# A fused chunk attention and two-layer MLP kernel: the first tile's reciprocals spread by fp32 TensorE transposes, its last k copies split over two engines

## The chip, the core and the metric

The kernel runs on one core of one Trainium2 chip. The time is device microseconds of one execution; "before" has a median of 291.13 us over the three runs that were there at the start (290.92 to 292.19).

## The reference, cut to what matters

```python
# q, k, v: 8 batches x 8 heads x 576 x 64, chunks of 64
scores = scale * q_c @ k_c.T            # within each chunk
attn = exp(scores - max); attn = attn / (attn.sum(-1) + 1e-9)
x = (attn @ v_c) -> (4608 tokens, 512)
out = gelu_exact(x @ w_in) @ w_out      # w_in 512 x 2048, w_out 2048 x 512
```

The tokens are worked through in nine tiles of 512. A tile has four "pairs" of heads (0 to 3). While one tile's MLP keeps TensorE busy, the attention of the next tile is slipped in between. Only the first tile's attention stands alone at the start, with nothing to hide behind.

## The kernel before

For one pair, the first tile does: transpose q and k; copy them out of PSUM, where the matmuls put their results (`qT`, and `k_bd`, a block-diagonal k in two halves of 64 partitions); scores `s_ps`; `pT = exp`; the sums of pT; their reciprocals, spread over 64 partitions each (`rc`); the product with v (`av_ps`); `x = av_ps * rc`. Then come the MLP's h slots: 16 slots of four matmuls each over x 0 to 3.

Pairs 0 and 1 get their reciprocals by VectorE, pairs 2 and 3 by TensorE:

```python
def att_sum(t, g, ...):                       # pairs 0, 1
    nc.tensor.matmul(sum_ps[:], ones_bd[:], pT[:], ...)
    nc.vector.transpose(t1, sum_ps)           # 32x32 blocks
    nc.vector.reciprocal(r1, t1[:, :, 0])
    nc.vector.transpose(rc, r1 broadcast)
def att_sum_pe(t, g):                         # pairs 2, 3
    for m in range(4):
        nc.tensor.matmul(sT[:, m], pT[..m..], ones_r[:], ...)    # sums, 2 columns
    nc.vector.reciprocal(rr[:], sT[:])
    def spread():                             # called later by the schedule
        for m in range(4):
            for r in range(2):
                nc.tensor.matmul(rc_ps[64*r:64*(r+1), m*128:(m+1)*128],
                                 rr[:, m, r:r+1].to_broadcast([128, 64]), ident_f[:],
                                 tile_position=(0, 64*r), ...)
        nc.scalar.copy(rc, rc_ps)
```

The schedule of the first tile is written out by hand (S_ scores, T transposes and copies, U reciprocals, A products with v, AC ScalarE, DV VectorE, PO GpSimd; `keep_warm(n)` issues n matmuls whose result nobody reads):

```python
S_[1]()
cast_qk(0, "q", 3, DV)
U[0]()
T[5](); T[6](); T[7]()          # k 2, q 3, k 3; k copied by AC
U[1]()
S_[2](); keep_warm(1); S_[3](); keep_warm(1)
p2 = att_sum_pe(0, 2); p3 = att_sum_pe(0, 3)
A[0](); p2(); A[1](); p3(); A[2](); keep_warm(1); A[3]()
# ... cut: loads
for i, eng in enumerate((PO, AC, DV, PO)):
    win[0](i, eng)              # casts of w_in for slots 0 to 3
act_table(Act.Gelu)
```

The whole kernel:

The softmax here doesn't subtract the row's maximum and nothing guards it: scores larger than these inputs give would overflow.

Of the kernel before, what the change touches and what calls it, by code (L numbers as in the profile page):

```python
# [11 lines left out]
def kernel(  # L12
# [137 lines left out]
        copy(qT[:].rearrange("p i (c j) -> p i c j", j=J), tp)  # L150
        tiles[t]["qT", g] = qT

    def att_Tk(t, g, copy):
        tp = transposed(t, "k", g)
        for r in range(2):
            sl = slice(CH * r, CH * (r + 1))
            copy(k_bds[g][sl, :, sl].rearrange("p i (c j) -> p i c j", j=J), tp[sl])  # L157


    def flip(t, nm):  # L160
# [101 lines left out]
    def att_sum_pe(t, g):  # L262

        pT = tiles[t]["pT", g]
        sT = ps_at.tile([P, MT // P, 2], f32, tag="at", name="sT")
        for m in range(MT // P):
            nc.tensor.matmul(sT[:, m], pT[:].rearrange("p i c -> p (i c)")[:, m * P:(m + 1) * P], ones_r[:],
                             start=True, stop=True)
        rr = work.tile([P, MT // P, 2], f32, tag="rr", name="rr", bufs=2)
        nc.vector.reciprocal(rr[:], sT[:])  # L270

        def spread():
            rc_ps = ps_mm.tile([P, MT], f32, tag="mm", name="rc_ps")
            for m in range(MT // P):
                for r in range(2):
                    nc.tensor.matmul(rc_ps[CH * r:CH * (r + 1), m * P:(m + 1) * P],  # L276
                                     rr[:, m, r:r + 1].to_broadcast([P, D]), ident_f[:],
                                     start=True, stop=True, tile_position=(0, CH * r))
            rc = work.tile([P, NB, 32], f32, tag="rc", name="rc", bufs=4)
            nc.scalar.copy(rc[:].rearrange("p n e -> p (n e)"), rc_ps[:])  # L280
            tiles[t]["rc", g] = rc
        return spread

# [17 lines left out]
    def att_units(t, cq=DV, ck=DV):  # L301
        tiles[t]["x"] = xpool.tile([P, G, MT], bf16, tag="x", name="x")
        T = []
        for g in range(G):
            T += [lambda g=g: att_Tq(t, g, cq), lambda g=g: att_Tk(t, g, ck if t == 0 or g < 2 else DV)]
        S_ = [lambda g=g: att_S(t, g) for g in range(G)]
        if t > 1:
            T = [lambda g=g: flip_k(t, g, ck) for g in range(G)]
            S_ = [lambda g=g: (att_S_flipped(t, g), att_part(t, g)) for g in range(G)]
        if t > 0:  # L310
            U = [lambda g=g: att_total(t, g, g + 2) for g in (0, 2)] + [lambda g=g: att_rc(t, g) for g in range(G)]
        else:
            U = [lambda g=g: att_sum(t, g) for g in range(G)]
        A = [lambda g=g: att_av(t, g) for g in range(G)]
        return T, S_, U, A
# [71 lines left out]
    def phase(t, extra1, extra2, by_rows=False, between={}):  # L387
        nms = MT // P
        order = [(ms, qt) for ms in range(nms) for qt in range(NQ)]
        if by_rows:  # L390
            order = [(None, f) for f in range(FF - FC)] + [(ms, NQ - 1) for ms in range(nms)]
        first = 3 if t == 1 else 1
        mm1_slot(t, 0, first, between)
        for f in range(first, FF):
            for u in extra1.get(f, ()):
                u()
            mm1_slot(t, f)
        for s, (ms, qt) in enumerate(order):
            for u in extra2.get(s, ()):
                u()  # L400
            if ms is None:
                mm2_rows(t, qt)
            else:
                mm2_slot(t, ms, qt)
        for u in extra2.get("end", ()):
            u()
# [43 lines left out]
    with tc.manual_schedule():  # L450
        for g in range(G):
            for nm in "qk":
                load_qk(0, nm, 2 * g, 2 * g + 2)
        load_v(0)
        win = [load_w_in(c, 2 if c < 2 else 1) for c in range(NWC - 1)]
        act_table(Act.Exp)
        keep_warm(7)
        zero_k(k_bds[0], nc.gpsimd)
        zero_k(k_bds[1], nc.gpsimd)
        zero_v(0, nc.vector)  # L460
        T, S_, U, A = att_units(0, DV, AC)
        cast_qk(0, "k", 0, PO)
        zero_k(k_bds[2], nc.gpsimd)
        cast_qk(0, "k", 1, PO)
        zero_k(k_bds[3], nc.gpsimd)
        cast_qk(0, "k", 2, PO)
        cast_qk(0, "k", 3, PO)
        for g in range(G):
            cast_v(0, 0, PO, slice(g, g + 1))
            cast_v(0, 1, PO, slice(g, g + 1))  # L470
        cast_qk(0, "q", 0, DV)
        T[0]()
        cast_qk(0, "q", 1, DV)
        T[1]()
        keep_warm(3)
        T[2]()
        S_[0]()
        T[3]()
        cast_qk(0, "q", 2, DV)
        keep_warm(1)  # L480
        T[4]()
        keep_warm(1)
        S_[1]()
        cast_qk(0, "q", 3, DV)
        U[0]()
        T[5]()
        T[6]()
        T[7]()
        U[1]()
        S_[2]()  # L490
        keep_warm(1)
        S_[3]()
        keep_warm(1)
        p2 = att_sum_pe(0, 2)
        p3 = att_sum_pe(0, 3)
        A[0]()
        p2()
        A[1]()
        p3()
        A[2]()  # L500
        keep_warm(1)
        A[3]()
        win.append(load_w_in(NWC - 1))
        wout = [load_w_out(0)]
        for i, eng in enumerate((PO, AC, DV, PO)):
            win[0](i, eng)
        act_table(Act.Gelu)
        load_qk(1, "q")
        wout.append(load_w_out(1))
        for c in range(1, NWC):  # L510
            for i in range(4):
                win[c](i, DV if i % 2 == 0 else PO)
            if c == 1:
                load_qk(1, "k")
            else:
                wout.append(load_w_out(c))
            if c < 3:
                r = slice(CH * (c - 1), CH * c)
                o = slice(CH * (2 - c), CH * (3 - c))
                nc.gpsimd.memset(v_bds[1][r, :, :, o], 0.0)  # L520
        for i in range(FC):
            wout[0](i, DV if i % 2 == 0 else PO)
        load_v(1)
        for g in range(G):
            cast_qk(1, "q", g, DV if g == 0 else PO)
        for i in range(FC):
            wout[1](i, DV if i % 2 == 0 else PO)
        for g in range(G):
            cast_qk(1, "k", g, DV if g % 2 == 0 else PO)
        for i in range(FC):  # L530
            wout[2](i, PO)
        for i in range(2):
            wout[3](i, PO)
        for g in range(G):
            for r in range(2):
                cast_v(1, r, PO, slice(g, g + 1))

        T, S_, U, A = att_units(1, AC, AC)
        def next_qk():
            for nm in "qk":  # L540
                load_qk(2, nm)
        over = []

        def sums():
            over.append(att_sums(1))
            over[0](1)
        phase(0, {}, {0: [lambda: act_table(Act.Exp)],
                      2: [T[0]], 3: [T[2]], 4: [T[4], T[6]], 7: [T[1], T[3]], 8: [T[5], S_[0]],
                      9: [T[7], S_[1], next_qk], 10: [S_[2], lambda: att_sum(1, 0), lambda: wout[3](2, DV)],
                      11: [lambda: wout[3](3, AC), S_[3]], 12: [sums],  # L550
                      13: [A[0], lambda: over[0](2), lambda: over[0](3), U[3]], 14: [A[1], U[4]], 15: [A[2], U[5]]},
              by_rows=True)
        last_av = {1: [A[3], lambda: rows_out(0, 3)]}
        pool_cast_qk(2)
        for t in range(1, NT):
            nxt = t + 1 < NT
            if nxt:
                T, S_, U, A = att_units(t + 1)
                for nm in "qk":
                    flip(t + 1, nm)  # L560
                if t == 1:
                    load_v(2)
                for r in range(2):
                    cast_v(t + 1, r, PO)
                if t + 2 < NT:
                    load_all(t + 2)
                    pool_cast_qk(t + 2)
            e1, e2 = {}, {}
            if nxt:
                e1 = {8: [T[0]], 10: [T[1]], 12: [T[2]], 14: [T[3]]}  # L570
                e2 = {0: [lambda: act_table(Act.Exp), S_[0]], 1: [S_[1]], 2: [S_[2]],
                      3: [S_[3], U[0]], 5: [U[1], lambda: act_table(Act.Gelu)],
                      7: [U[2], A[0]], 8: [U[3], A[1]], 10: [U[4], A[2]], 12: [U[5], A[3]]}
            phase(t, e1, e2, between=last_av if t == 1 else {})
# [28 lines left out]
```

## Time and profile before

| | before |
|---|---|
| time, median | 291.13 us |
| TensorE busy | 278.2 us, 96% of the span |
| score matmuls of pair 1 begin ("S1") | 9.42 us |
| scores of pair 3 begin | 12.77 us |
| x of pair 3 done | 18.52 us |
| long run of h matmuls begins | 18.56 us, 3 of 64 done |

The last four rows are from TensorE's and VectorE's timelines.

### The profile page before, as it was taken

How to read it: one execution, taken by the hardware profiler on the slowest of the kernel's cores; microseconds unless marked ns; L12 is line 12 of the kernel's file. 1: busy time of each engine (PE TensorE's matmuls, PEld its weight loads, DVE VectorE, ACT ScalarE, POOL GpSimd, SP SyncE). 2: the span in 40 equal slices, each digit the busy share in tenths (PEclk: the TensorE clock that was granted, in tenths of full speed). 3: DMA queues.
4: the chain of work that ended last, by engine and by line, in shares of the span. 5: the costliest groups of instructions: out<-in, count | busy, mean ns of one | idle time of the engine just before them, and what ended most of it. 6: DMA issues, size and time to landing. Idle time of an engine off the chain costs nothing.

```text
span 288.9 us, 4859 instructions
## 1 busy us (share of the span) xinstructions
PE 278.2 (96%) x1836; PEld 138.5 (48%) x1870; DVE 154.8 (54%) x265; ACT 170.1 (59%) x329; POOL 98.8 (34%) x136
## 2 busy tenths in 40 slices
PE   7699999999999999999999999999999999999994
PEld 2454455445544554455445544554455445544444
DVE  6854349348805882749246935394268425850011
ACT  3767766967447844785468536763785368626400
POOL 6859758605651830262008400650003610000000
PEclk9999999999999999999999999999999999999999
DMA  6999999999799726961698259914999970120033
GB/s 222 247 360 404 393 337 265 254 207 286 191 291 311 168 99 161 325 145 74 161 261 234 76 138 285 233 73 115 163 130 131 265 147 2 39 106 2 0 73 73
DMA packets 96887, 53.79 MB, mean 186 GB/s; under 512 B 68576, under 2 KB 89312, under 8 KB 96864
## 3 DMA queue, kind: packets, MB, share of 16 engines
q1 hardware_dynamic: 96704, 53.36, 69.8%
q8 instruction: 14, 0.23, 0.3%
q10 hardware_dynamic: 160, 0.13, 0.2%
q14 instruction: 9, 0.07, 0.1%
HBM read 36.70 MB, written 9.44 MB: 160 GB/s over the span
## 4 chain that ended last, share of the span: by engine, by line
PE 90%; DVE 3%; ACT 3%; DMA 2%; issue 1%; SPq 0%; POOL 0%; DVEq 0%; POOLq 0%
PE h_ps L328 42%; PE y_ps L344 37%; PE av_ps L289 3%; PE y_ps L384 3%; PE s_ps L180 2%; DMA arrival<-in_k_dram 2%; ACT k_bd L157 2%; PE y_ps L369 1%; DVE x L296 1%; PE tp L144 1%; PE rc_ps L276 1%; DVE rc L259 1%; ACT pT L194 1%; SPq L112 0%; PE s_ps L192 0%
## 5 line engine op out<-in xcount | busy, mean ns | idle before, releaser
L328 PE MATMUL h_ps<-x,w_in_sb 128*128 128x512 bf16 x565 | 125.8, 379 | 1.0 <-DVE x L296 0.4
L331 ACT ACTIVATE h<-h_ps 128x512 bf16<-128x512 f32 x144 | 85.5, 597 | 62.5 <-PE h_ps L328 62.4
L344 PE MATMUL y_ps<-w_out_sb,h 128*128 128x512 bf16 x493 | 117.9, 379 | 0.9
L328 PEld LDWEIGHTS <-w_in_sb 128*128 128x128 bf16 x576 | 56.2, 98 | 68.4 <-issue 1.2
L344 PEld LDWEIGHTS <-h 128*128 128x128 bf16 x512 | 46.0, 98 | 46.5 <-issue 0.2
L172 DVE COPY k_bd<-k_t 64x512 bf16<-64x512 bf16 x56 | 35.6, 636 | 53.6 <-DMA k_t<-k_nat 52.6
L133 POOL CAST q_nat<-arrival 128x512 bf16<-128x512 f32 x31 | 21.2, 720 | 95.0 <-DMA arrival<-in_q_dram 95.0
L137 POOL CAST v_bd<-arrival 64x512 bf16<-64x512 f32 (+1 forms) x30 | 36.3, 1210 | 20.5 <-DMA arrival<-in_v_dram 13.3
L296 DVE TENSOR_TENSOR x<-av_ps,rc 128x512 bf16<-128x512 f32 x36 | 24.8, 692 | 4.7 <-PE av_ps L289 1.4
L133 POOL CAST k_nat<-arrival 128x512 bf16<-128x512 f32 x34 | 20.1, 625 | 11.2 <-DMA arrival<-in_k_dram 9.2
L448 ACT ACT_TABLE_LOAD x18 | 23.1, 1283 | 1.0 <-PEq L587 0.7
L353 DVE COPY y_sb<-y_ps 128x512 f32<-128x512 f32 x11 | 7.6, 691 | 29.7 <-PE y_ps L344 27.8
L353 ACT COPY y_sb<-y_ps 128x512 f32<-128x512 f32 x24 | 13.8, 580 | 14.7 <-PE y_ps L344 14.4
L239 DVE STREAM_TRANSPOSE pt<-pT 128x256 f32<-128x256 f32 x28 | 12.2, 437 | 18.8 <-ACT pT L183 18.8
L259 DVE STREAM_TRANSPOSE rc<-rb 128x512 f32<-128x512 f32 x31 | 21.5, 692 | 0.2 <-ACT rb L229 0.2
L242 DVE TENSOR_REDUCE part<-pt 128x16 f32<-128x512 bf16 x28 | 19.2, 686 | 1.0
L250 ACT COPY other<-part 32x32 f32<-32x32 f32 x56 | 12.0, 215 | 10.4 <-DVE part L242 9.9
L289 PEld LDWEIGHTS <-v_bd 128*128 128x128 bf16 x288 | 13.0, 98 | 8.0 <-issue 0.3
L183 ACT ACTIVATE pT<-s_ps 128x512 bf16<-128x512 f32 x28 | 14.7, 590 | 0.0
L289 PE MATMUL av_ps<-pT,v_bd 128*128 128x64 bf16 x288 | 14.3, 193 | 0.2
L180 PEld LDWEIGHTS <-k_bd 128*128 128x128 bf16 x224 | 10.4, 98 | 6.6
L384 PE MATMUL y_ps<-w_out_sb,h 128*128 128x512 bf16 x46 | 11.9, 379 | 0.4 <-ACT h L331 0.3
(68 smaller groups left out, 136.5 us busy)
## 6 DMA issues: line engine op xcount, KB each, us to landing
arrival<-in_v_dram SPq DMA_DIRECT2D x72, 128.0 KB, 4.1
out_dram<-y_sb SPq DMA_DIRECT2D x32, 256.0 KB, 2.3
arrival<-in_q_dram SPq DMA_DIRECT2D x7, 1024.0 KB, 6.7
arrival<-in_k_dram SPq DMA_DIRECT2D x7, 1024.0 KB, 9.1
arrival<-in_moe_w_out_dram SPq DMA_DIRECT2D x4, 1024.0 KB, 12.2
arrival<-in_moe_w_in_dram SPq DMA_DIRECT2D x4, 512.0 KB, 6.2
arrival<-in_moe_w_in_dram SPq DMA_DIRECT2D x2, 1024.0 KB, 10.4
arrival<-in_q_dram SPq DMA_DIRECT2D x4, 256.0 KB, 4.7
```

The source lines that it names most:

```text
L133: copy(st[nm][:, g].rearrange("p j r d -> p r j d"), st[nm + "f"][:, 2 * g:2 * g + 2])
L137: copy(v_bds[t % NV][sl, :, gs, sl].rearrange("p i g d -> p g i d"), tiles[t]["vf"][sl, gs])
L172: copy(k_bds[g][sl, :, sl].rearrange("p i (c j) -> p i c j", j=J), src[sl])
L259: nc.vector.transpose(rc[:], src.to_broadcast([P, NB, 32]))
L289: nc.tensor.matmul(av_ps[:, i, :], v_bds[t % NV][:, i, g, :], st["pT", g][:, i, :], start=True, stop=True)
L296: nc.vector.tensor_tensor(x, av, rc, op=mybir.AluOpType.mult)
L328: nc.tensor.matmul(h_ps[a][:], w_in_sb[:, ks, (f + a) * P:(f + a + 1) * P], st["x"][:, ks, :], start=(ks == 0), stop=(ks == KS - 1))
L331: nc.scalar.activation(st["h"][:, f + a, :], h_ps[a][:], Act.Gelu)
L344: nc.tensor.matmul(y_ps[:], st["h"][:, f, ms * P:(ms + 1) * P], w_out_sb[:, f, :], start=(f == 0), stop=(f == FF - 1))
L353: (AC if ms < 3 and t + 1 < NT else DV)(y_sb[:], y_ps[:])
L384: nc.tensor.matmul(tiles[t]["y_ps", ms][:], tiles[t]["h"][:, f, ms * P:(ms + 1) * P], w_out_sb[:, f, :], start=(f == 0), stop=False)
L448: nc.scalar.activation(act_scratch[:], rest[:, 0:1], func)
```

## The change

All four pairs get their sums from TensorE and spread their reciprocals by transposes of a broadcast; VectorE is freed of four stream transposes. k copies 2 and 3 are split between ScalarE and VectorE. Two warm-up matmuls go, and the first two h slots are opened together so that TensorE has six h matmuls, not three, before it needs x 3. Cut from the diff: the spreads of pairs 2 and 3 take their PSUM buffer from another pool.

```diff
-            copy(k_bds[g][sl, :, sl]..., tp[sl])
+            copies[r](k_bds[g][sl, :, sl]..., tp[sl])      # (AC, DV) for pairs 2, 3
...
-                for r in range(2):
-                    nc.tensor.matmul(rc_ps[CH*r:CH*(r+1), m*P:(m+1)*P],
-                                     rr[:, m, r:r+1].to_broadcast([P, D]), ident_f[:],
-                                     start=True, stop=True, tile_position=(0, CH*r))
+                for r in (1, 0):
+                    nc.tensor.transpose(flat[0:CH*(r+1), m*P:(m+1)*P],
+                                        rr[:, m, r:r+1].to_broadcast([P, CH*(r+1)]), ident_f[:])
...
-        first = 3 if t == 1 else 1
+        first = (2, 3, 1)[min(t, 2)]
...
-        U[0]()
+        p0 = att_sum_pe(0, 0)
         T[5]()
+        p0()
         T[6]()
         T[7]()
-        U[1]()
+        p1 = att_sum_pe(0, 1)
         S_[2]()
+        p1()
         keep_warm(1)
         S_[3]()
-        keep_warm(1)
         p2 = att_sum_pe(0, 2)
+        p2()
+        A[0]()
+        A[1]()
         p3 = att_sum_pe(0, 3)
-        A[0](); p2(); A[1](); p3(); A[2](); keep_warm(1); A[3]()      (one line each)
+        p3()
+        A[2]()
+        A[3]()
...
-        for i, eng in enumerate((PO, AC, DV, PO)):
+        act_table(Act.Gelu)
+        for i, eng in enumerate((PO, DV, DV, PO)):
             win[0](i, eng)
-        act_table(Act.Gelu)
```

More of the change, by code (lines that the diff above doesn't have):

```diff
@@ L151, in att_Tq, with att_Tk @@
         tiles[t]["qT", g] = qT
-    def att_Tk(t, g, copy):
+    def att_Tk(t, g, copies):
         tp = transposed(t, "k", g)
@@ L156, in att_Tk @@
             sl = slice(CH * r, CH * (r + 1))
-            copy(k_bds[g][sl, :, sl].rearrange("p i (c j) -> p i c j", j=J), tp[sl])
+            copies[r](k_bds[g][sl, :, sl].rearrange("p i (c j) -> p i c j", j=J), tp[sl])
     def flip(t, nm):
@@ L272, in spread @@
         def spread():
-            rc_ps = ps_mm.tile([P, MT], f32, tag="mm", name="rc_ps")
+            pool, tag = (ps_mm, "mm") if g < 2 else (ps_tp, "tp")
+            rc_ps = pool.tile([P, NB, 32], f32, tag=tag, name="rc_ps")
+            flat = rc_ps[:].rearrange("p n e -> p (n e)")
             for m in range(MT // P):
-                for r in range(2):
-                    nc.tensor.matmul(rc_ps[CH * r:CH * (r + 1), m * P:(m + 1) * P],
-                                     rr[:, m, r:r + 1].to_broadcast([P, D]), ident_f[:],
-                                     start=True, stop=True, tile_position=(0, CH * r))
+                for r in (1, 0):
+                    nc.tensor.transpose(flat[0:CH * (r + 1), m * P:(m + 1) * P],
+                                        rr[:, m, r:r + 1].to_broadcast([P, CH * (r + 1)]), ident_f[:])
             rc = work.tile([P, NB, 32], f32, tag="rc", name="rc", bufs=4)
-            nc.scalar.copy(rc[:].rearrange("p n e -> p (n e)"), rc_ps[:])
+            nc.scalar.copy(rc[:], rc_ps[:])
             tiles[t]["rc", g] = rc
@@ L304, in att_units @@
         for g in range(G):
-            T += [lambda g=g: att_Tq(t, g, cq), lambda g=g: att_Tk(t, g, ck if t == 0 or g < 2 else DV)]
+            T += [lambda g=g: att_Tq(t, g, cq), lambda g=g: att_Tk(t, g, (AC, DV) if t == 0 and g > 1 else [AC if t == 0 or g < 2 else DV] * 2)]
         S_ = [lambda g=g: att_S(t, g) for g in range(G)]
@@ L484 @@
         cast_qk(0, "q", 3, DV)
-        U[0]()
+        p0 = att_sum_pe(0, 0)
         T[5]()
+        p0()
         T[6]()
         T[7]()
-        U[1]()
+        p1 = att_sum_pe(0, 1)
         S_[2]()
+        p1()
         keep_warm(1)
         S_[3]()
-        keep_warm(1)
         p2 = att_sum_pe(0, 2)
+        p2()
+        A[0]()
+        A[1]()
         p3 = att_sum_pe(0, 3)
-        A[0]()
-        p2()
-        A[1]()
         p3()
         A[2]()
-        keep_warm(1)
         A[3]()
```

## The prediction

> **What bounds the kernel now.** I read the page first, then the stages, then the chain of work that ended last over the first 45 us, then each engine's timeline up to the first large matmul. The page of the kernel before:
>
> ```profile
> PE 278.2 (96%) x1836; PEld 138.5 (48%) x1870; DVE 154.8 (54%) x265; ACT 170.1 (59%) x329; POOL 98.8 (34%) x136
> ...
> PE   7699999999999999999999999999999999999994
> ```
>
> TensorE is busy 96% of the span, and only the first three slices of 7.2 us are under 9 tenths: all its slack lies before about 20 us. The code of the change lies there too (first tile's attention and its first h slots). After that the kernel is a conveyor of matmuls: TensorE's waits from 70 us on come to nothing in the view of waits, and those from 18.6 to 70 us come to 0.9 us. So a shift of the moment at which the large matmuls begin should arrive at the end almost whole, in either direction, and the change can be worth no more than its effect on that moment. The chain between 7 and 19 us shows what sets it:
>
> ```profile
> 8.79 0.59 ACT k_bd L157
> 9.38 0.05 issue
> 9.42 0.42 PE s_ps L192 x8
> 9.85 0.02 issue
> 9.87 0.60 ACT pT L194
> 10.46 0.46 ACT k_bd L157
> ...
> 12.74 1.09 ACT pT L194 x2
> 13.83 0.05 issue
> 13.88 0.25 PE sT L267 x4
> 14.13 0.26 PE av_ps L289 x8
> 14.38 1.02 PE rc_ps L276 x16
> 15.41 0.34 PE av_ps L289 x8
> 15.75 1.02 PE rc_ps L276 x16
> ...
> 17.83 0.69 DVE x L296
> 18.52 0.04 issue
> 18.56 8.36 PE h_ps L328 x38
> ```
>
> Columns: start, length, engine, tile. ScalarE is the bottleneck from 9.9 to 13.8 (four k copies of 0.58 us between exponentials), then TensorE with two spreads of 1.02 us each, then the product x of pair 3. TensorE's timeline shows what it already did by then:
>
> ```profile
> 17.40 0.94 PE L328 MATMUL h_ps<-x,w_in_sb 128*128 128x512 bf16 x3
> 18.56 13.32 PE L328 MATMUL h_ps<-x,w_in_sb 128*128 128x512 bf16 x60 [0.22 <-DVE x L296]
> ```
>
> Three of the 64 h matmuls (those of x 0 to 2 of the first slot) ran before x 3 was there. The other 61 follow at 0.216 us each (8.36/38 is 0.22) without a wait of size.
>
> **What the Trainium skill says.** "TensorE: Matmul & The Clock Gate", Terms, says that trn2's transpose mode is 4 times faster for FP32; no trace before has an fp32 transpose, so this is a hope. The same page, LDWEIGHTS, gives columns/1.2 ns per weight load; the trace agrees: 16 loads of 64 fp32 columns took 0.85 us, 53 ns each. "TensorEngine Tiling (Array Packing)", Restrictions, says that column tiling disables the FP32 transpose mode, which is why the new code writes all 128 rows and then overwrites the upper 64. "PSUM — Partial Sum Buffer", Engine vs sequencer instructions: VectorE and ScalarE queues are strict FIFO and matmuls start in program order. The trace agrees: the two reciprocals of pairs 2 and 3 waited behind a stream transpose until 13.99, though the first sT was issued at 13.39. Nearly all of my estimate comes from this last point.
>
> **The change part by part.**
> (a) Spreads. Before: two, each 8 fp32 matmuls, run as 16 passes in 1.02 us. After: four, each 4 transposes of 128 columns and 4 of 64. Estimate from the page's load rate: 4 x (107 + 53) ns = 0.64 us if the loads alone set it; single passes that don't overlap their loads would give 1.1 us. I take 0.75 us. TensorE: 4 x 0.75 against 2 x 1.02, so 1.0 us more.
> (b) VectorE loses two stream-transpose pairs and one reciprocal for pairs 0 and 1 (0.72 + 0.25 + 0.71 us each, less a new reciprocal of 0.19: 3.0 us together) and gains two k copies (0.70 us each by its four at 41.14 us).
> (c) ScalarE loses two k copies (1.16 us) and gains two rc copies (0.58 each): no change in sum, but pairs 2 and 3 of k are no longer four in a row.
> (d) Slot f=1's weights are cast by VectorE, not ScalarE, and two h slots are opened together.
>
> Now the order. Comparing both builds' instruction orders, VectorE has in the new one: q cast 3, rr0, k copy 2, qT3, k copy 3, rr1, rr2, x0, x1, **rr3**, x2, x3, then the casts of w_in. TensorE has: S1, sT0, T k2, **p0**, T q3, T k3, sT1, S2, **p1**, warm, S3, sT2, **p2**, A0, A1, sT3, **p3**, A2, A3, h (p is a spread, A the product with v). Each p waits for its reciprocal, and everything after p waits for p. With durations from the trace (4 transposes 0.22 issued and 0.44 to the reader, S 0.23 and 0.45, A 0.34 and 0.45, qT 0.69, x 0.69 with 0.60 spacing):
> - S1 at 9.42 as before, sT0 9.64, k2 transposed 9.76 (read at 10.20). rr0 ends 10.16. p0 10.22 to 10.97. q3 transposed 10.97, k3 11.19 (k3's cast ends 11.03, a DMA arrival that doesn't move). qT3 11.41 to 12.10, k copy 3 on VectorE to 12.75, **rr1 12.94**. S2 runs at 11.5.
> - p1 12.98 to 13.73: TensorE has idled since S2. The warm matmul to 13.95, S3 13.95. Before, S3 ran at 12.77. ScalarE: rc1 13.83 to 14.41, pT3 14.41 to 15.00, against 13.83 before.
> - sT2 14.18, rr2 to 14.62, p2 14.65 to 15.40, A0 and A1 to 16.08, sT3 to 16.19. x0 15.85 to 16.54, x1 to 17.14. Only then rr3, to **17.32**: TensorE idles 1.1 us again. p3 17.36 to 18.11, A2 and A3 to 18.79 (rc3 also 18.79). x2 18.56, x3 ends 19.85. Before, 18.52.
> - The opened pair: the second h matmul needs slot 1's weights, whose cast stands behind x3 on VectorE. It takes 0.43 us (0.70 where a POOL cast runs beside it, as at 18.42 before; "SBUF — State Buffer", Who interferes with whom, has the two sharing a port). So one h matmul runs early instead of three, and the conveyor starts at about 20.30 with 63 left.
>
> Sum: (20.30 + 63 x 0.216) - (18.56 + 61 x 0.216) = 1.74 + 0.43 = **2.2 us later**, less a little that later waits may take up. 291.13 + 2.1 = 293.2.
>
> **The rivals.**
> (1) The change does what it is for: k copies in parallel, VectorE relieved, no ScalarE row of four. For it: k3 is complete at 12.75 with ScalarE free earlier, and 3.0 us of VectorE work is gone. If p1 and p3 didn't wait, S3 would run at 12.8 and the end would be POOL's: v casts to 16.28, w_in slice 0 to 16.95, A3 near 16.6, x3 near 17.4, the cast of slice 1 to 17.9. That is 0.2 us better at most, so 291. Against it: the FIFO orders above.
> (2) The fp32 transposes cost more than the matmuls, as multi-pass work without column tiling: 1.3 us each. Three stand on the path, and p0 delays k3 as well, so each 0.25 us more on a spread is about 1.0 us: about 295.4. Against it: the "4 times faster" line.
> (3) They cost 0.5 us: about 292.3.
> (4) A transfer hides it: weights or k3 might be what is waited for anyway. For it: k3's cast is bound by arrival (0.84 us idle). Against it: TensorE's matmuls from 18.56 wait for no DMA, so a late start uses no slack.
>
> **Range and chances.** The working gives 293.2. The spread's length moves it by -1 to +2, and a wait misjudged by half a microsecond, together with the runs' own scatter (290.92 to 292.19), by about 0.8. Rival 1 sets the low end a little under 291.4. I give 291.3 to 295.0. 2% is 5.8 us; no rival reaches it, since the whole stage that is changed lasts only some 10 us and a gain is capped by POOL: faster 0.01, same 0.96, slower 0.03.
>
> **What would show it.** In the changed trace: x of pair 3 ending near 19.8 (before 18.52); TensorE idle before p1 and p3, released by VectorE's reciprocal, about 1.1 us each; rr3 starting just when x1 ends; rc_ps groups of 0.6 to 1.1 us; one h matmul, then a wait for VectorE's w_in cast, then an unbroken run; TensorE's busy time up by about 1 us or less (two warm matmuls fewer). Wrong, if S3 starts before 13 us, if p3 starts with x0, or if the conveyor starts late but the end doesn't move, which would mean a slack after 20 us that I have not seen.

## More of the kernel before

S1 is a good zero for comparing kernels: nothing before it is changed, but it moves with the arrival of q and k.

A plain difference of two profiles mixes that in, so times since S1 are used further on.

## The result and the profile after

The changed kernel takes 294.56 us (median of 4, 294.26 to 294.83) against 291.02 us of the kernel before in the same rounds: 3.5 us more. The ratio is 1.0114, with an interval from 1.0084 to 1.0144. (A ratio here is the mean time of one kernel's fast runs over that of the other's of the same rounds, so it is not quite the ratio of the medians that are quoted.) It is slower, by less than 2%.

The page of the changed kernel, the busy times and TensorE's slices:

```profile
PE 281.5 (96%) x1874; PEld 140.6 (48%) x1874; DVE 155.0 (53%) x264; ACT 169.5 (58%) x328; POOL 98.7 (34%) x136
...
PE   7669999999999999999999999999999999999994
```

Only the third slice shows a change (6 in place of 9). From the fourth on the conveyor is as full as before. The granted clock is 1.00 in every 5 us stretch from 5 to 25 us, so the two warm-up matmuls that went did not lower it. The chain of work that ended last, from 12.8 to 22 us (start, length, engine, tile), answers to the chain of before in the prediction:

```profile
12.77 0.48 ACT k_bd L157
13.25 0.02 issue
13.28 0.71 DVE k_bd L157
13.98 0.02 issue
14.00 0.22 DVE rr L270
14.22 0.04 issue
14.27 1.09 PE rc_ps L280 x8
15.35 0.21 PE warm L446
15.57 0.23 PE s_ps L192 x8
...
16.18 1.09 PE rc_ps L280 x8
...
18.15 0.68 DVE x L299
18.83 0.13 DVE rr L270
18.95 0.04 issue
19.00 1.09 PE rc_ps L280 x8
20.09 0.25 PE av_ps L292 x8
...
21.03 0.68 DVE x L299
21.71 0.34 DVE w_in_sb L427
22.06 0.05 issue
22.11 13.79 PE h_ps L331 x63
```

Read it backwards. The run of 63 h matmuls starts when VectorE has cast slot 1's weights (21.71 to 22.06). That cast stood behind x 3, which needs spread 3 (19.00). That spread needs the reciprocal at 18.83, and the reciprocal stood behind x 1 (18.15 to 18.83). Further up, spread 1 (14.27) needs reciprocal 1 (14.00), which stood behind VectorE's half of k copy 3 (13.28). TensorE's own timeline shows the three holes, each with its releaser in brackets:

```profile
12.53 0.39 PE L192 MATMUL s_ps<-qT,k_bd 128*128 128x64 bf16 x8
14.27 1.09 PE L280 MATMUL rc_ps<-ident_f,rr 128*128 128x128 f32 x8 [1.34 <-DVE rr L270]
15.19 0.38 PE L446 MATMUL warm<-rest 128*128 128x512 bf16 x1
15.40 0.40 PE L192 MATMUL s_ps<-qT,k_bd 128*128 128x64 bf16 x8
...
17.57 0.24 PE L267 MATMUL sT<-ones_r,pT 128*128 128x2 bf16 x4
19.00 1.09 PE L280 MATMUL rc_ps<-ident_f,rr 128*128 128x128 f32 x8 [1.19 <-DVE rr L270]
19.92 0.63 PE L292 MATMUL av_ps<-pT,v_bd 128*128 128x64 bf16 x16
20.39 0.38 PE L331 MATMUL h_ps<-x,w_in_sb 128*128 128x512 bf16 x1
22.11 4.06 PE L331 MATMUL h_ps<-x,w_in_sb 128*128 128x512 bf16 x18 [1.34 <-DVE w_in_sb L427]
```

1.34 us before spread 1, 1.19 us before spread 3, 1.34 us before the second h matmul. VectorE is not overworked; the instruction that TensorE waits for merely stands behind others in its queue. And the split copy shows in ScalarE's and VectorE's timelines:

```profile
11.08 0.57 ACT L157 COPY k_bd<-tp 64x512 bf16<-64x512 bf16 x1
12.66 0.58 ACT L157 COPY k_bd<-tp 64x512 bf16<-64x512 bf16 x1
```

```profile
11.68 0.69 DVE L157 COPY k_bd<-tp 64x512 bf16<-64x512 bf16 x1 [0.67 <-ACT k_bd L157]
12.40 0.69 DVE L150 COPY qT<-tp 128x512 bf16<-128x512 bf16 x1
13.28 0.69 DVE L157 COPY k_bd<-tp 64x512 bf16<-64x512 bf16 x1 [0.18 <-ACT k_bd L157]
14.00 0.21 DVE L270 RECIPROCAL rr<-sT 128x8 f32<-128x8 f32 x1
```

VectorE's half begins when ScalarE's half ends (11.65 and 13.24), both times, and the profile names ScalarE's half as the releaser. The two halves of one copy run one after the other, here and in the nine other profiles that have the split; what in the built program asks for this order (the shared source or the shared target tile) no run shows.

### The profile page after: what moved, and what is told of

It is laid out like the page before. It is cut to its first block, busy times and chain, and to the rows that moved or that the text cites. A ratio compares the mean times of both kernels' runs of the same rounds, so it can differ in the third digit from the quotient of the medians.

```text
span 293.0 us, 4901 instructions
## 1 busy us (share of the span) xinstructions
PE 281.5 (96%) x1874; PEld 140.6 (48%) x1874; DVE 155.0 (53%) x264; ACT 169.5 (58%) x328; POOL 98.7 (34%) x136
## 4 chain that ended last, share of the span: by engine, by line
PE 90%; DVE 3%; DMA 2%; ACT 1%; SPq 1%; issue 1%; DVEq 0%
PE h_ps L331 42%; PE y_ps L347 37%; PE y_ps L387 3%; PE av_ps L292 2%; DMA arrival<-in_q_dram 2%; PE s_ps L180 2%; PE rc_ps L280 1%; DVE x L299 1%; PE y_ps L372 1%; SPq L112 1%; DVE rc L259 1%; PE tp L144 1%; ACT k_bd L157 1%; PE s_ps L192 0%; ACT rb L229 0%
## 5 line engine op out<-in xcount | busy, mean ns | idle before, releaser
L347 PE MATMUL y_ps<-w_out_sb,h 128*128 128x512 bf16 x512 | 120.5, 379 | 0.0
L387 PE MATMUL y_ps<-w_out_sb,h 128*128 128x512 bf16 x48 | 12.0, 379 | 0.3 <-ACT h L334 0.3
```

Source lines behind the costliest of these rows:

```text
L347: nc.tensor.matmul(y_ps[:], st["h"][:, f, ms * P:(ms + 1) * P], w_out_sb[:, f, :], start=(f == 0), stop=(f == FF - 1))
L387: nc.tensor.matmul(tiles[t]["y_ps", ms][:], tiles[t]["h"][:, f, ms * P:(ms + 1) * P], w_out_sb[:, f, :], start=(f == 0), stop=False)
```

## The experiments

**The theories.** Mine: the loss is three waits that come from the order of instructions on VectorE (reciprocal 1 behind the k copies, reciprocal 3 behind x 1, slot 1's cast behind x 3), so moving single instructions gives it back. First rival: the loss is the amount of TensorE work (four fp32 spreads in place of two); then the order would hardly matter. Second rival: transfers arrive late. Third: the split copy is the useful part, and the rest spoils it.

Each run below had 5 timed rounds; the kernel before had medians of 291.02, 291.21 and 291.18 us. The intervals of the ratio of e1, e6 and e8 lie clear below that of the changed kernel (1.0084 to 1.0144); those of e2, e3 and e4 overlap it, so for these three the size rests on the trace.

**e1: reciprocal 1 earlier.**

```diff
         p0()
+        p1 = att_sum_pe(0, 1)
         T[6]()
         T[7]()
-        p1 = att_sum_pe(0, 1)
         S_[2]()
```

> The changed kernel with one move: sT1 and its reciprocal (pair 1) come right after the spread of pair 0, so that the reciprocal stands ahead of qT3 and k copy 3 on VectorE. Waiting theory: spread 1 starts about 1.3 us earlier, the scores of pair 3 start with k copy 3 (about 14.0 us in the changed kernel's own times, not 15.4), and the whole comes out about 1.4 us under the changed kernel's 294.56: 293.2. Rival (the four fp32 spreads are simply more TensorE work): the same spreads run, so no change above 0.3 us.

292.79 us, ratio 1.0052. The wait is gone from TensorE's timeline; the spread follows the scores at once:

```profile
11.94 0.41 PE L192 MATMUL s_ps<-qT,k_bd 128*128 128x64 bf16 x8
12.18 1.08 PE L280 MATMUL rc_ps<-ident_f,rr 128*128 128x128 f32 x8
```

That is 1.8 us off by the medians, 1.4 us by the time from S1 to the long run of h. The rival (no change above 0.3 us) falls: the same spreads ran.

**e2: reciprocal 3 earlier.**

```diff
+        p3 = att_sum_pe(0, 3)
         A[0]()
         A[1]()
-        p3 = att_sum_pe(0, 3)
         p3()
```

> The changed kernel with one move: sT3 and its reciprocal come before the two products with v of pairs 0 and 1, so that the reciprocal stands ahead of x 0 and x 1 on VectorE. Waiting theory: TensorE's idle 1.2 us before spread 3 goes, about 1.25 us off: 293.3. Rival (amount of TensorE work): no change above 0.3 us.

293.63 us, ratio 1.0084: 0.9 us off by the medians, 1.5 us since S1. The hole before spread 3 is gone:

```profile
16.68 0.63 PE L292 MATMUL av_ps<-pT,v_bd 128*128 128x64 bf16 x16
17.15 1.07 PE L280 MATMUL rc_ps<-ident_f,rr 128*128 128x128 f32 x8
```

Direction and size fit within the scatter of the runs (292.94 to 294.46).

**e3: slot 1's slice cast on ScalarE, ahead of its table load.**

```diff
-        act_table(Act.Gelu)
-        for i, eng in enumerate((PO, DV, DV, PO)):
+        for i, eng in enumerate((PO, AC, DV, PO)):
             win[0](i, eng)
+        act_table(Act.Gelu)
```

> The changed kernel with slot 1's w_in slice cast on ScalarE again (ahead of its table load), two h slots still opened together. Waiting theory: the 1.3 us wait of the second h matmul ends at about 21.35 us of the changed kernel's time and not at 22.1, 0.75 us off: 293.8. If the opened pair cost nothing: no change.

292.94 us (292.50 to 294.33), ratio 1.0073. More than expected by the medians (1.6 us), near it since S1 (1.0 us). S1 lies early in this profile, at 9.39 us. The wait before the second h matmul is 0.73 us in place of 1.34, now for ScalarE:

```profile
20.40 6.87 PE L331 MATMUL h_ps<-x,w_in_sb 128*128 128x512 bf16 x31 [0.73 <-ACT w_in_sb L427]
```

**e4: one slot opened.**

```diff
-        first = (2, 3, 1)[min(t, 2)]
+        first = (1, 3, 1)[min(t, 2)]
```

> The changed kernel with one h slot opened, as before; slot 1's weights still cast by VectorE after x 3. Waiting theory: three h matmuls run before x 3 in place of one, and one more beside the cast, 3 x 0.216 = 0.65 us off: 293.9. If the opened pair was a gain: slower than 294.56.

293.85 us, ratio 1.0098: 0.7 us off by the medians, 0.9 us by the trace (below the table), as expected. By the trace, opening two slots cost time here, because the second slot's weights were not cast.

**e5: all four spreads by the earlier matmuls.**

```diff
-                for r in (1, 0):
-                    nc.tensor.transpose(...)
+                for r in range(2):
+                    nc.tensor.matmul(..., tile_position=(0, CH * r))
```

> The changed kernel with all four spreads done by the earlier fp32 matmuls with column tiles in place of transposes, everything else kept. Waiting theory: the way of spreading is a small term; 0.92 us for the transposes against 1.02 us for the matmuls, four on or near the path: 0.3 to 0.4 us slower than the changed kernel, about 294.9. Rival (fp32 transposes are what costs): 1 us or more faster than 294.56.

295.15 us, ratio 1.0129: 0.6 us slower by the medians, 0.3 us since S1. A spread occupies TensorE for 1.02 us (10.59 to the next block at 11.61 in its timeline) against 0.92 us for the transposes (11.06 to 11.98 in the changed kernel). So by the trace the transposes are the shorter way, by 10% of a spread; the timed intervals of the two kernels overlap (1.0107 to 1.0151 and 1.0084 to 1.0144) and don't tell them apart. The transposes are not what costs: the rival of 1 us or more faster falls.

**e6: k copies on ScalarE alone.**

```diff
-att_Tk(t, g, (AC, DV) if t == 0 and g > 1 else [...] * 2)
+att_Tk(t, g, [AC if t == 0 or g < 2 else DV] * 2)
```

> The changed kernel with both halves of k copies 2 and 3 on ScalarE again. The trace of the changed kernel shows the halves one after the other (VectorE's begins when ScalarE's ends), so two engines do not shorten a copy; and VectorE's half stands ahead of the reciprocal of pair 1. Theory: that reciprocal comes after qT3 alone, spread 1 starts about 1.1 us earlier, about 1.1 us off: 293.4. Rival (the split is the useful part of the change): ScalarE is the bottleneck again, 0.5 us or more slower than 294.56.

292.76 us, ratio 1.0059: 1.8 us off by the medians and 1.0 us since S1. Undoing the split is a gain. VectorE's halves no longer stand ahead of reciprocal 1 (spread 1 waits 0.24 us in place of 1.34), and ScalarE's two halves in a row take no longer than ScalarE's and VectorE's one after the other. e1 and e6 remove the same wait in two ways, so their gains should not add; no run has both.

**e7: the kernel before with transposes in its two spreads.**

```diff
-                for r in range(2):
-                    nc.tensor.matmul(rc_ps[...], ..., tile_position=(0, CH * r))
+                for r in (1, 0):
+                    nc.tensor.transpose(rc_ps[0:CH * (r + 1), ...], ..., ident_f[:])
```

> The kernel before with one part of the change alone: its two spreads done by transposes. Theory: 2 x 0.10 us off the path, 290.8. If transposes cost TensorE more than their length shows (a mode change): slower than 291.0 by 0.2 us or more.

291.52 us (290.21 to 292.32), ratio 1.0008, interval 0.9983 to 1.0033: no difference can be told, neither the 0.2 us hoped for nor the 0.2 us feared. The trace shows a gain in front, but then something new. The chain that ended last, from 14.9 us on:

```profile
14.93 9.76 DMA arrival<-in_moe_w_in_dram
24.69 0.02 issue
24.71 0.44 DVE w_in_sb L423
25.15 0.05 issue
25.20 6.87 PE h_ps L327 x31
```

The 33rd h matmul (slot 8, the first of w_in's third quarter) now starts on the arrival of its weights, at 25.20 us, 0.4 us after it was due (17.87 + 32 x 0.216 = 24.78). In the kernel before, that quarter's first VectorE cast began at 23.75 us, about 1.1 us ahead of the 24.82 us at which its slot was due (29 matmuls of 0.216 us after 18.56); the cast itself takes some 0.44 of that. The earlier front is only half of the matter. Counted since S1, slot 8 was due 0.5 us earlier in e7 (14.93 against 15.40), but its weights also arrived 0.5 us later (14.86 against 14.33), although the edit leaves the loads alone.

**e8: e1, e2 and e3 together.**

> The changed kernel with the three moves together (reciprocals 1 and 3 earlier, slot 1's slice cast on ScalarE). If the three waits are the whole loss and add up: 1.4 + 1.5 + 0.9 = 3.8 us off, about 290.8, unless GpSimd's casts of v (to about 16.3 us) and of the first w_in slice (to about 16.95) become the next wait; then 291.0 to 291.5. Rival (the added TensorE work of 1.6 us, two more spreads at 0.92 less two warm matmuls, is the loss): it stays at 292.5 or above.

291.14 us (290.35 to 292.68), ratio 1.0008. The three moves give back 3.4 us, all that the change had lost, with the four spreads still in it. So the added TensorE work is not the loss: the rival (292.5 or above) falls. What that work costs by itself and what the freed VectorE gives, no run separates. Nothing beyond is won. A possible reason is in its trace, which is of the slowest of its six executions (292.68 us). TensorE's first h matmul, and GpSimd's cast that released it:

```profile
18.60 4.74 PE L331 MATMUL h_ps<-x,w_in_sb 128*128 128x512 bf16 x21 [0.69 <-POOL w_in_sb L427]
```

```profile
17.93 0.61 POOL L427 CAST w_in_sb<-arrival 128x512 bf16<-128x512 f32 x1 [0.48 <-DMA arrival<-in_moe_w_in_dram]
```

In this execution the front waits for the first w_in slice's arrival. But SyncE began to issue the w_in loads, which the edits leave alone, at 13.02 us here and at 11.92 in the profile of the kernel before. So whether the faster executions of e8 wait for an arrival too is not shown.

**e9, e10, e11: the loads thinned, wrong results.** The first tile's v of pairs 2 and 3 isn't loaded, which takes four issues out of the queue ahead of w_in (relative error 0.335).

```diff
-        load_v(0)
+        load_v(0, range(2))
...
-        copy(v_bds[...], tiles[t]["vf"][sl, gs])
+        copy(v_bds[...], tiles[t]["vf"][sl, slice(gs.start % 2, gs.start % 2 + 1) if t == 0 else gs])
```

> Wrong result on purpose: the kernel with all three moves, in which the first tile's v of pairs 2 and 3 is not loaded (the casts read the v of pairs 0 and 1), so the queue has four issues of some 0.88 us less before the w_in loads and w_in lands earlier. Its first h matmul then waited 0.7 us for a w_in cast that waited for its arrival, and a later one 0.3 us. Floor theory (with the waits gone, the arrival of w_in binds): about 0.7 to 1 us faster than the 291.14 of the same kernel with all loads, 290.3. Rival (TensorE's added spreads bind): no change.

290.64 us, ratio 0.9995 (0.9972 to 1.0017). The waits for an arrival are gone, but the second h matmul then waited 0.73 us for ScalarE's cast of slot 1. 0.5 us off e8 is inside the scatter, so this run doesn't settle how much the arrivals alone hold back.

> Control, wrong result on purpose: the changed kernel with the same loads left out. Its conveyor starts behind a chain of reciprocals and x, not behind an arrival: no change above 0.4 us from 294.56 (fewer bytes may let k and q land a little earlier). Rival (the change is slow because transfers arrive late): 1 us or more faster.

294.35 us (294.11 to 298.31): no change, and TensorE waits 1.30 and 1.19 us before spreads 1 and 3, as in the changed kernel. So late transfers are not why the changed kernel is slow. Its trace adds a detail. w_in being early, GpSimd's memset came early too, and VectorE's cast of slot 1 ran beside it from 21.04 us; TensorE resumed only at 22.18:

```profile
20.04 1.80 POOL L523 MEMSET v_bd<- 64x2048 bf16 x1
```

The same cast took 0.43 us in the changed kernel. "SBUF — State Buffer", section Who interferes with whom, in the Trainium skill calls this an exclusive lock on a port pair that VectorE and GpSimd share; here the run shows about 1.1 us in place of 0.43. So this control has a new cost of some 0.7 us in its last wait, which may hide a gain of that size, though not the rival's 1 us.

> Control, wrong result on purpose: the kernel before with the same loads left out. In its trace the w_in arrivals had up to 1 us of slack, so 0 to 0.5 us off 291.0. 1 us or more off would say that the kernel before was already bound by the arrival of w_in in most runs.

291.58 us, ratio 1.0030 (1.0003 to 1.0057): no gain. Alone, that does not show that the arrival of w_in leaves the kernel before free, for the same new cost appears here: in the profiled execution (293.5 us, the slowest of six) GpSimd's memset began at 20.26 us, VectorE cast beside it, and TensorE waited.

```profile
20.26 1.80 POOL L520 MEMSET v_bd<- 64x2048 bf16 x1
```

```profile
22.40 0.82 PE L328 MATMUL h_ps<-x,w_in_sb 128*128 128x512 bf16 x3 [0.96 <-DVE w_in_sb L424]
```

What speaks for it is the trace of the kernel before: from 18 to 60 us TensorE's waits, 0.9 us in all, are for x, h and k, none for w_in. The profile of e11 shows another thing: q of pair 1 arrived late, TensorE waited 1.7 us, and its granted clock fell. The columns are the stretch in us, its length, the busy time of each engine, then the clock, DMA share and GB/s:

```profile
7.00:9.00 2.00, 0.93 (x14) 0.78 (x15) 1.16 (x3) 0.35 (x1) 0.82 (x2) 0.79 1.10 361
9.00:11.00 2.00, 2.00 (x16) 1.15 (x15) 1.18 (x3) 1.40 (x3) 1.54 (x3) 0.50 0.80 187
```

**e12: an attempt to beat both.** e8, with the first half of w_in's first quarter issued from GpSimd's queue.

```diff
+        held[0]()                  # nc.gpsimd.dma_start of w_in chunk 0, first half
         cast_qk(0, "k", 3, PO)
```

> Correct result, an attempt to beat both: all three moves, and the first half of w_in chunk 0 issued from GpSimd's queue in front of the cast of k 3 (where GpSimd waits about 1 us for an arrival), so that this half and all later loads of the other queue start 0.85 us earlier. Floor theory: 0.5 to 0.8 us off 291.14, 290.5, if GpSimd's own issue costs no more than its idle time; if it costs more, GpSimd's casts of v move and it is 291 or above.

291.65 us, ratio 1.0027. A miss. w_in came earlier, but v came later: GpSimd waited 0.33 and 0.71 us for arrivals of v, and the last product with v waited 0.41 us for its cast. The DMA share was 1.05 or more in every 5 us stretch from 5 to 25 us (0.70 in e8's from 10 to 15), so one transfer's gain was probably another's loss. No version here clearly beats the kernel before.

**All runs.** S1 and the run of h are from each profile, which is a single execution; "after S1" is their difference.

| run | median us | ratio to before | S1 | long run of h | after S1 |
|---|---|---|---|---|---|
| before | 291.02 | 1 | 9.42 | 18.56, 3 done | 9.14 |
| changed | 294.56 | 1.0114 | 10.14 | 22.11, 1 done | 11.97 |
| e1 | 292.79 | 1.0052 | 9.65 | 20.18, 1 done | 10.53 |
| e2 | 293.63 | 1.0084 | 9.75 | 20.23, 1 done | 10.48 |
| e3 | 292.94 | 1.0073 | 9.39 | 20.40, 1 done | 11.01 |
| e4 | 293.85 | 1.0098 | 9.87 | 21.36, 3 done | 11.49 |
| e5 | 295.15 | 1.0129 | 9.80 | 22.05, 1 done | 12.25 |
| e6 | 292.76 | 1.0059 | 8.93 | 19.93, 1 done | 11.00 |
| e7 | 291.52 | 1.0008 | 9.85 | 17.87, none | 8.02 |
| e8 | 291.14 | 1.0008 | 10.07 | 18.60, none | 8.53 |

"Done" counts the h matmuls before the run by program order; a few of their records are missing from the traces. Each one done is worth 0.216 us, which makes e4's gain 0.48 + 0.43 = 0.9 us since S1.

## Why the prediction was right, and where its sizes were off

The prediction was right in direction and mechanism and inside its range, and short in size: it worked out 2.2 us and the medians show 3.5 us. Counted since S1, the changed kernel's h run starts 2.83 us later (11.97 against 9.14) with two matmuls fewer done (0.43 us), together 3.26 us; the rest, 0.3 us, is within the interval of the ratio, and no run pins it down.

- "Everything after p waits for p", reciprocal 1 behind k copy 3: right. The hole is 1.34 us; e1 takes it away and e6 all but 0.24 us of it.
- Reciprocal 3 "starting just when x1 ends": right, 18.75 us while x 1 ends at 18.83, a hole of 1.19 us (1.1 predicted); e2 takes it away.
- "One h matmul runs early instead of three", with a 0.43 us cast behind x 3: right, 0.43 us; by the trace e3 and e4 each give back about the expected part.
- "A shift ... should arrive at the end almost whole": right. From 22 to 70 us the changed kernel's TensorE has, besides the w_in cast wait, the same small waits as before.
- **The mis-sized term is (a), "I take 0.75 us" for a spread.** It occupied 0.92 us. On p1, p2 and p3 this is 3 x 0.17 = 0.51 us. p0 started 0.12 us later since S1 than in my walk and was 0.17 us longer, which pushed q3 and k3 by 0.29 us. My own rule (0.25 us more on a spread is about 1.0 us) gives 0.7 us for 0.17.
- **The other is k copy 3 "on VectorE to 12.75"**, which took the halves as parallel. VectorE's half was free to begin when qT3 ended (12.40 + 0.69 = 13.09) and began at 13.28, when ScalarE's had ended: 0.19 us more. The three, 0.51 + 0.29 + 0.19 = 0.99 us, are most of the 1.14 us by which x 3 was later than predicted (11.57 since S1 against 19.85 - 9.42 = 10.43).
- Rival 1 said that even without the waits the change could gain 0.2 us at most, for GpSimd's casts. e8, equal to the kernel before, fits such a bound; in its one profile, a slow execution, the cast of slice 0 itself waited for w_in's arrival. Rival 4 (a transfer hides it) was rightly set aside for the changed kernel (e10); in the profiles of e7 and e8 TensorE did wait for an arrival, part of it because the weights came later there.
- "4 times faster" did not show in the length of a spread: rivals 2 and 3, at 1.3 and 0.5 us a spread, both fell.
- Two readings of the page were off, without harm to the argument. In the page of the kernel before, only the first two slices (and the last) are under 9 tenths, not the first three. And the sign "TensorE's busy time up by about 1 us or less" was not met: 278.2 to 281.5 us. But the page of the kernel before has 1836 matmul records for 1870 weight loads, so its busy time is too short by an unknown amount, and the sign settles nothing.

Open: whether e8 is held by the arrival of w_in in most executions, how fast it would be with w_in always there in time (e9 left a new wait in its place), and how much of the scatter of S1 each timed run had.

## What to carry to other kernels

Moving work to an idle engine helps only if the small result that another engine waits for does not stand behind large independent work in that engine's queue: before a reorder, write each engine's new order down and look at what precedes every producer of a wait. After splitting one copy over two engines, look at what releases each half; here the halves ran in turn. And when a front becomes shorter, ask which transfer it will meet: in the kernel before, w_in's third quarter was cast about 0.6 us before its slot was due, and its arrival since S1 differed by as much between single profiles.

## What the Trainium skill lacked or had wrong

- "TensorE: Matmul & The Clock Gate", Terms, says that transpose mode is 4 times faster for FP32. Here a spread by 8 fp32 transposes occupied TensorE for 0.92 us against 1.02 us for 8 fp32 matmuls run as 16 passes: 10%. The two are not the same work (the transposes load 768 columns, the matmuls 1024 in their 16 loads), so this does not test the factor itself. A transpose record is as long as a pass of the fp32 matmul (273 ns median each). No page gives the time of an fp32 transpose.
- The same page, LDWEIGHTS, gives columns/1.2 ns, from which 4 x (107 + 53) = 0.64 us of loads for a spread is estimated. The 8 loads extended over 0.82 us in the trace and the spread over 0.92 us, so the loads' rate alone didn't set it.
- The same page, Why this matters for your kernels, warns of TensorE idle gaps over about 3 us. In e11's profile the clock was 0.79 from 7 to 9 us and 0.50 from 9 to 11 us around a single wait of 1.7 us, in a stretch that was already thinly filled (TensorE was busy 1.04 us of the 2 us before it). In e8 a wait of 1.29 us at the same place left the clock at 1.00.
- "PSUM — Partial Sum Buffer", PSUM bank collisions raise a hardware error, says that two engines may use different partition quadrants of one bank at the same time. It doesn't say that a kernel's build may order them anyway: VectorE's half began at 11.68 us, when ScalarE's, on other partitions, had ended at 11.65. Whether the PSUM source or the target tile was the cause is not shown.
